# Spectral filter and ELU block on one core: order of the first loads, and new places for weight conversion and sums of x

## The chip, the cores and the metric

One core of a Trainium2 chip. The metric is the device time of one execution in microseconds (us). Engines: PE (TensorE), DVE (VectorE), ACT (ScalarE), POOL (GpSimd), SP (SyncE, which here only issues DMAs).

## The reference, cut to what matters

```python
X = np.fft.rfft(x, axis=1)                  # x: (8, 3008, 256) float32
Y = X * (filt_r + 1j * filt_i)[None]        # filter: (1505, 256)
x = np.fft.irfft(Y, n=3008, axis=1).reshape(24064, 256)
h = x @ w_in                                # w_in: (256, 2048)
g = np.where(h > 0, h, np.exp(np.minimum(h, 0)) - 1)
return g @ w_out                            # w_out: (2048, 256)
```

The weights arrive as 64-bit floats and are turned into float32 by the kernel itself.

## The kernel before, in words

The transforms are matmuls with tables: 3008 = 47 x 64, so a first pass over 64 points (tables `ta`, `tf`), a product with the filter, and the way back (`gs`, `t8`, `tn`). The two weight matrices are used in a seven-product scheme for 2x2 blocks, so sums of weight blocks are needed as well as the blocks.

**Batch 0, up to about 96 us**, has code of its own (L826 to L923). x comes in six pieces `xs[0, c]` (`x_load_first`, L269, SP's queue; pieces 4 and 5 lie in buffers of the pool `t1p`); the table of pieces 2 and 3, and that of 4 and 5, come in one load each. `a_first` (L279) makes the first pass of a piece, `t_first` (L294) transposes for group g of 8, `b_first` (L356) makes group g's spectrum and `products` (L348) multiplies it with the filter `ff` on DVE, `bi_first` (L370) goes back, `y_write_first` (L387) writes to DRAM, and two reads (`y_read_first`, L396) bring it back as `t4f` for `n_first` (L526). The filter is read by `f_read_first` (L323) in four parts: (0,0) and (1,0) on SP's queue, (0,1) and (1,1) on POOL's; groups 0 to 3 need (0,*), groups 4 to 7 (1,*).

**Weights** come in 16 pieces of 512 KB (`w_fetch`, L735), pieces 4q to 4q+3 being quarter q, first two of w_in, then two of w_out. A piece k is converted by `w_split(k)` (two DVE instructions), `w_float(k)` (four ACT instructions, or those numbered: the first needs only the piece, the others the split) and `w_join(k)` (three or four DVE instructions); `w_sums` (four instructions) makes the block sums of a half quarter, on DVE or POOL. `step(k)` is split, float and the join of k-1. The temporary for piece k is `wtmp[WTMP[k]]`. Pieces 5 to 7 are converted beside the filter's groups by the table `BESIDE` (L896): its entry g is put behind group g.

**The rest** is a loop over quads, i = 0, 1, ... (L1025): a quad is one (batch, piece m, weight quarter q) with seven steps up (`up_steps`: matmuls with w_in, copies and ELU) and, for the quad before it, seven down (`down_steps`: matmuls with w_out). The quads start in the order (0,0,0), (0,0,1), (0,1,0..3), (0,0,2), (0,0,3), so quarter q = 1 is needed in quad 1, q = 2 in quad 4, q = 3 in quad 5 (w_out one quad later). Everything else is hung into this loop by hand with `at(quad, place, function, ...)`: place 2 is behind the third step of the first half, place 0 between the halves, place 3 inside the second half, place 1 at the end. Program order is the order in each engine's queue, and no engine passes over a waiting instruction.

Hung in there: pieces 8 to 15 of the weights; `x_load` (SP), `x_unit` (sum and difference of a piece of x, on POOL for batch 1, L223), `a_unit` (the matmuls on them, L234); `f_arrange` (a rearranged copy of the filter in DRAM); `n_unit` and `n_sums` (the last pass and its sums on DVE); `c_unit`, `c_last`, `c_part`, `o_unit` (joining and writing output, DVE and SP).

The steps of piece 4 stand in the code before the first `t_first`:

```python
            step(4)
            w_join(4)
            for k in (5, 6, 7):
                w_fetch(k)
```

Of the kernel before, what the change touches and what calls it, by code (L numbers as in the profile page):

```python
# [32 lines left out]
XC = 4  # L33
# [3 lines left out]
FBUFS = 3  # L37
XSUMS = 6
SUMS = 4
WTMP = (0, 1, 2, 3, 0, 1, 0, 1, 2, 3, 2, 3, 2, 3, 2, 3)  # L40
LO, HI = slice(0, 48), slice(64, 112)
HALVES = slice(0, 64), slice(64, 128)

# [95 lines left out]
def kernel(  # L139
# [47 lines left out]
    edges = glob.tile([P, 2], FP32, name="edges")  # L187
# [547 lines left out]
    def w_fetch(k, queue=nc.gpsimd):  # L735
        q, j = divmod(k, 4)

        if k in (3, 4):
            wd = xp.tile([P, 2, 2, D], FP32, tag="xc", name="wd").rearrange("p k u d -> p (k u d)")
        elif k in (8, 9):  # L740
            wd = t2[:, k - 8].rearrange("p u d -> p (u d)")
        elif k == 13:
            wd = t3s["first"][:, 0].rearrange("p u d -> p (u d)")
        elif k == 15:
            wd = op.tile([P, 16, 2, 32], FP32, tag="o", name="wd").rearrange("p j e s -> p (j e s)")
        else:
            wd = fbufs[{5: 0, 6: 1, 7: 2, 10: 0, 11: 1, 12: 2, 14: 2}.get(k, k)].rearrange("p c u d -> p (c u d)")
        wd = wds[k] = wd.bitcast(U32).rearrange("p (a w) -> p a w", w=2)
        if j < 2:
            srcs = [moe_w_in.bitcast(U32)[ts(j, P), ts(q, 1024)]]  # L750
        else:
            srcs = [moe_w_out.bitcast(U32)[ts(4 * q + 2 * (j - 2) + i, P), :] for i in range(2)]
        for i, s in enumerate(srcs):
            n = 512 // len(srcs)
            queue.dma_start(wd[:, ts(i, n), :].rearrange("p a w -> p (a w)"), s)
# [67 lines left out]
    with tc.manual_schedule():  # L823


        with tc.tile_pool(name="boot", bufs=1) as bp:  # L826
# [18 lines left out]
            for c in (2, 3):  # L845
                x_load_first(c)
            w_fetch(2, nc.sync)
            for c in (4, 5):
                x_load_first(c)
            for z in zt[0] + zt[1]:  # L850
                nc.gpsimd.memset(z.rearrange("p (k r) -> p k r", r=ROWS)[:, :, 48:64], 0.0)
            for gh in range(2):
# [12 lines left out]
            def step(k):  # L865
                w_split(k)
                w_float(k)
                if k > 0:
                    w_join(k - 1)

            nc.sync.dma_start(once, once_d)
            nc.sync.dma_start(gs, gs_d)
            step(0)
            a_first(0)
            step(1)
            a_first(1)
            w_fetch(3)
            w_fetch(4)
            f_read_first(0, 0, nc.sync)
            f_read_first(0, 1, nc.gpsimd)  # L880
            a_first(2)
            step(2)
            a_first(3)
            t4f = xp.tile([P, 2, 2, D], FP32, tag="xc", name="t4f").rearrange("p k u d -> p (k u) d")
            f_read_first(1, 0, nc.sync)
            f_read_first(1, 1, nc.gpsimd)
            step(3)
            a_first(4)
# [41 lines left out]
        n_first(t8)  # L930
        tn_read(0, 1)
        y_read(0, 1)
        for k in (8, 9):
            w_fetch(k, nc.sync)
        for c in range(2):
            x_load(1, c)
        for k in (10, 11, 12, 13):
            w_fetch(k, nc.sync)
        w_fetch(15, nc.sync)

# [6 lines left out]
            plan.setdefault((quad, place), []).append((fn, a))  # L947


        for quad, place, fn, *a in ((0, 0, w_split, 8), (0, 1, w_float, 8),  # L950
                                    (1, 2, w_join, 8), (1, 2, w_split, 9), (1, 0, w_float, 9), (1, 1, w_join, 9),
                                    (1, 1, w_split, 10), (2, 0, w_float, 10),
                                    (2, 1, w_join, 10), (2, 1, w_split, 11), (3, 2, w_float, 11),
                                    (3, 0, w_join, 11), (3, 0, w_split, 12), (3, 1, w_float, 12),
                                    (3, 1, w_join, 12), (4, 2, w_split, 13), (4, 2, w_float, 13), (4, 0, w_join, 13),
                                    (4, 0, w_split, 14), (4, 0, w_float, 14), (4, 1, w_join, 14),
                                    (5, 2, w_split, 15), (5, 2, w_float, 15), (5, 0, w_join, 15),
                                    (1, 1, w_sums, 9, nc.gpsimd), (3, 0, w_sums, 11, nc.gpsimd),
                                    (4, 0, w_sums, 13, nc.gpsimd), (5, 0, w_sums, 15, nc.gpsimd),
                                    (3, 1, w_fetch, 14)):  # L960
            at(quad, place, fn, *a)
        for c in range(2, XBUFS):
            at(c - 2, 0, x_load, 1, c)
# [8 lines left out]
        for b in range(B):  # L972
            t = (b - 1) * PER
            if b > 0:
                for c, s in enumerate((2, 2, 3, 3, 4, 4) if b == 1 else (0, 0, 3, 3, 4, 4)):
                    at(t + s, 0, x_unit, b, c)
# [19 lines left out]
            for m, (s, place, sums) in enumerate(((23, 2, ((23, 0, 0, 1), (23, 3, 2))), (25, 1, ((25, 1),)), (29, 1, ((29, 1),)),  # L996
                                                   (32, 0, ((33, 1),)), (36, 0, ((37, 1),)), (40, 0, ((41, 1),)))):
                if (b, m) == (0, 1):
                    at(0, 1, n_unit, 0, 1)
                    at(0, 1, n_sums, 0, 1)  # L1000
                elif b > 0 or m > 0:
                    r = 21 if m == 0 else s - 2
                    at(t + r, 0, tn_read, b, m)
                    at(t + r, 1 if m == 0 else 0, y_read, b, m)
                    at(t + s, place, n_unit, b, m)

                    for q, p, *a in sums:
                        at(t + q, p, n_sums, b, m, *a)
                if (b, m) == (0, 0):
                    at(3, 0, c_unit, 0, 0)  # L1010
                    at(3, 0, c_last, 0, 0)
                    at(9, 2, c_unit, 0, 0)
                    at(9, 0, c_last, 0, 0)
                    at(9, 0, c_part)
                    at(10, 0, o_unit, 0, 0)
                elif (b, m) == (0, 1):
                    at(7, 0, c_unit, 0, 1)
                    at(8, 0, o_unit, 0, 1)
# [6 lines left out]
        for i in range(-PER, len(items) + 3):  # L1025
# [3 lines left out]
            for n, k in enumerate("DUUDUDDU" if i in opens else "UUDUDDU"):  # L1029
                s = ups if k == "U" else downs  # L1030
                if s:
                    s.pop(0)()
                if n == 2:
                    for fn, a in plan.get((i, 2), ()):
                        fn(*a)
            for fn, a in plan.get((i, 0), ()):
                fn(*a)
# [45 lines left out]
```

## Time and profile before

| what | us |
|---|---|
| three runs: median (lowest to highest) | 2591.99 (2590.68 to 2596.08) |
| profiled execution: its own time | 2595.79 |
| its span, first to last instruction | 2594.0 |
| PE busy of the span | 2526.7 (97%) |
| DVE, ACT, POOL busy | 2064.4, 1538.1, 179.4 |
| 0 to 96 us: PE busy, mean DMA rate | 57.53, 179 GB/s |
| 96 to 196 us: PE busy, DVE busy | 84.44, 76.80 |
| 196 to 250 us: PE busy | 50.69 |

Busy PE is the time in which a matmul is in flight. DMA queue q1 is SP's, q0 POOL's. In timelines a row has start and length in us, engine, line, operation, output<-inputs, shape, and in brackets the idle time of the engine before it and what ended it.

### The profile page before, as it was taken

The numbers are of one execution on the slowest core, as the hardware profiler recorded it, in microseconds if no ns is written. First come the engines' busy times: TensorE is split into PE (matmuls) and PEld (weight loads), VectorE is DVE, ScalarE is ACT, GpSimd is POOL, SyncE is SP. The second block draws the span as 40 slices with busy tenths as digits, with TensorE's granted clock in tenths as the row PEclk, the third lists the DMA queues.
The fourth block names the chain that finished last, engine by engine and source line by source line (L and its number), as shares of the span: only waits on it lengthen the run. The fifth ranks groups of instructions, "written<-read, shape, count | busy, mean of one in ns | idle before, by whom it ended". The sixth has DMA issues, their size and how long they took to land.

```text
span 2594.0 us, 44154 instructions
## 1 busy us (share of the span) xinstructions
PE 2526.7 (97%) x16726; PEld 2161.7 (83%) x16726; DVE 2064.4 (80%) x3609; ACT 1538.1 (59%) x2714; POOL 179.4 (7%) x314
## 2 busy tenths in 40 slices
PE   5889999999999999999999999999999999999998
PEld 4568888888898888988889888898888888898887
DVE  4778887788877888778887888878887788866766
ACT  4575565666556655566556655566556656555554
POOL 3050000001000100000000000000010001000000
PEclk8999999999999999999999999999999999999999
DMA  8662313432135222342314332253313232120010
GB/s 198 186 174 61 82 35 75 120 81 63 28 83 138 68 56 47 87 119 59 76 41 117 81 74 57 50 141 69 72 48 76 72 77 68 31 50 18 19 27 17
DMA packets 228738, 197.23 MB, mean 76 GB/s; under 512 B 128852, under 2 KB 202294, under 8 KB 228334
## 3 DMA queue, kind: packets, MB, share of 16 engines
q1 hardware_dynamic: 215118, 167.42, 26.7%
q0 software_dynamic: 12256, 26.73, 3.9%
q8 instruction: 132, 2.16, 0.4%
q14 instruction: 80, 0.66, 0.1%
q10 hardware_dynamic: 1152, 0.26, 0.1%
HBM read 122.46 MB, written 74.97 MB: 76 GB/s over the span
## 4 chain that ended last, share of the span: by engine, by line
PE 88%; DVE 5%; ACT 2%; DMA 2%; issue 1%; SPq 0%; POOL 0%; DVEq 0%; POOLq 0%; ACTq 0%
PE po L667 41%; PE phs L584 23%; PE phd L584 11%; PE pha L584 6%; PE pse L512 2%; PE pf L411 1%; PE psa L241 1%; PE pv L477 1%; DMA x<-in_x_dram 1%; DVE g L592 1%; DVE g L606 1%; ACT e L602 1%; ACT e L601 1%; DMA t<-tf_t 0%; DMA ff<-in_filt_i_dram 0%
## 5 line engine op out<-in xcount | busy, mean ns | idle before, releaser
L667 PE MATMUL po<-g,wo 128*128 128x256 f32 (+1 forms) x5376 | 1316.9, 377 | 0.0
L667 PEld LDWEIGHTS po<-g,wo 128*128 128x128 f32 x5376 | 1013.7, 190 | 165.4 <-issue 49.7
L595 ACT ACTIVATE g<-phs 128x512 f32<-128x512 f32 (+1 forms) x576 | 338.7, 588 | 717.6 <-PE phs L584 716.6
L584 PE MATMUL phs<-y,wi 128*128 128x256 f32 (+1 forms) x2288 | 580.6, 376 | 5.3 <-ACT g L595 5.3
L602 ACT ACTIVATE e<-e 128x512 f32<-128x512 f32 (+1 forms) x768 | 477.2, 621 | 24.4
L584 PEld LDWEIGHTS phs<-y,wi 128*128 128x128 f32 x2288 | 430.0, 190 | 60.6 <-ACT g L595 8.1
L592 DVE TENSOR_TENSOR g<-phd,g 128x512 f32<-128x512 f32 (+1 forms) x384 | 259.3, 675 | 268.7 <-ACT e L602 196.4
L606 DVE SCALAR_TENSOR_TENSOR g<-e,g 128x512 f32<-128x512 f32 (+1 forms) x576 | 389.4, 676 | 1.5 <-ACT e L602 1.1
L601 ACT ACTIVATE e<-g 128x512 f32<-128x512 f32 (+1 forms) x576 | 353.5, 614 | 62.1 <-DVE g L592 51.1
L606 DVE SCALAR_TENSOR_TENSOR g<-e,phs 128x512 f32<-128x512 f32 (+1 forms) x192 | 129.8, 676 | 145.4 <-ACT e L602 145.4
L584 PE MATMUL phs<-ys,wi 128*128 128x256 f32 (+1 forms) x784 | 198.9, 376 | 4.7 <-ACT g L595 4.7
L584 PE MATMUL phd<-y,wi 128*128 128x256 f32 (+1 forms) x768 | 194.7, 376 | 5.6 <-DVE g L592 5.6
L584 PE MATMUL phd<-ys,wi 128*128 128x256 f32 (+1 forms) x768 | 193.8, 375 | 0.0
L584 PE MATMUL pha<-ys,wi 128*128 128x256 f32 (+1 forms) x752 | 190.0, 375 | 0.0
L601 ACT ACTIVATE e<-phs 128x512 f32<-128x512 f32 (+1 forms) x192 | 113.4, 591 | 112.0 <-PE phs L584 112.0
L584 PEld LDWEIGHTS phs<-ys,wi 128*128 128x128 f32 x784 | 147.8, 190 | 23.2 <-ACT g L595 6.3
L584 PEld LDWEIGHTS phd<-y,wi 128*128 128x128 f32 x768 | 145.0, 190 | 25.5 <-DVE g L592 9.5
L584 PEld LDWEIGHTS phd<-ys,wi 128*128 128x128 f32 x768 | 145.8, 190 | 16.7 <-DVE g L592 0.2
L340 POOL DMA_DIRECT2D fall<-fp x224 | 110.0, 499 | 693.1 <-DVE r L450 690.4
L584 PEld LDWEIGHTS pha<-ys,wi 128*128 128x128 f32 x752 | 142.8, 190 | 16.5
L592 DVE TENSOR_TENSOR g<-pha,g 128x512 f32<-128x512 f32 (+1 forms) x192 | 129.3, 674 | 23.4 <-PE pha L584 23.4
L643 DVE TENSOR_TENSOR g<-g,g 128x512 f32<-128x512 f32 (+1 forms) x192 | 131.7, 686 | 6.7
(181 smaller groups left out, 2163.9 us busy)
## 6 DMA issues: line engine op xcount, KB each, us to landing
t<-yd SPq DMA_DIRECT2D x94, 256.0 KB
z<-t SPq DMA_DIRECT2D x84, 256.0 KB
fall<-fp POOLq DMA_DIRECT2D x224, 96.0 KB, 2.9
t<-z SPq DMA_DIRECT2D x224, 96.0 KB
yd<-t SPq DMA_DIRECT2D x112, 192.0 KB
out_dram<-o SPq DMA_DIRECT2D x632, 32.0 KB
xc<-in_x_dram SPq DMA_DIRECT2D x84, 128.0 KB
xc<-in_x_dram SPq DMA_DIRECT2D x161, 64.0 KB
```

The lines of the kernel that those rows point to most:

```text
L241: nc.tensor.matmul(p[o:o + 64, u, :], w[r, u, o:o + 64], src[r, u, :], start=True, stop=True)
L340: nc.gpsimd.dma_start(t[32 * a:32 * a + 24].rearrange("p c u d -> p (c u d)"), fp[g, a].rearrange("q c u d -> q (c u d)"))
L411: nc.tensor.matmul(pf[p][1][32 * a:32 * a + 32, js, :], fb[r, v, :], t2[r, js, a, :], start=True, stop=True, tile_position=(32 * p, 32 * a))
L512: nc.tensor.matmul(p[o:o + 64, dh, ds(64 * q, n)], t[r, i - 4 * m, ds(dh * P + o, 64)], w[r, i - 4 * m, 0:n], start=True, stop=True)
L584: nc.tensor.matmul(ps[:, a, 0:h], w_in[q][:, COMBO[n], a, :], y[n], start=start and a == 0, stop=True, skip_group_check=True)
L592: nc.vector.tensor_tensor(out=g[o], in0=i0, in1=i1, op=ALU.add)
L595: nc.scalar.activation(out=g[o], in_=i0, func=AXT.Copy)
L601: nc.scalar.activation(out=e, in_=src, func=AXT.Relu, scale=-1.0)
L602: nc.scalar.activation(out=e, in_=e, func=AXT.Exp, scale=-1.0)
L606: nc.vector.scalar_tensor_tensor(out=g[n], in0=es[n], scalar=1.0, in1=src, op0=ALU.subtract, op1=ALU.max)
L643: nc.vector.tensor_tensor(out=b12, in0=b22, in1=b12, op=ALU.subtract)
L667: nc.tensor.matmul(po[i][:, u, 0:h], w_out[q][:, COMBO[n], a, :], g[n][:, a, :], start=begin and a == 0 and n in (1, 3, 6, 4), stop=True, ...
```

## The change

On **POOL**, a copy of one element per partition of x piece 4 is put ahead of POOL's parts of the filter; piece 4 of the weights is fetched behind those, and piece 8 is new behind 5 to 7. On **SP**, piece 3 of the weights and x piece 5 follow x piece 4 and stand ahead of `once`, `gs` and SP's parts of the filter. Piece 4 is converted beside the filter's groups, 5 and 6 later there, 7 and 8 behind them: so pieces 0 to 3 are converted ahead of the filter and 8 ahead of the quads. After the filter SP fetches 9 and 10, two pieces of x, then 11 to 15. In the quads there is a new place 4 (behind step 5, or 4 where a quad starts with a down step), floats are split over places, `x_unit` of batch 1 is called a quad earlier, the sums of piece 15 are on DVE, and some sums and output steps have other places.

```diff
-WTMP = (0, 1, 2, 3, 0, 1, 0, 1, 2, 3, 2, 3, 2, 3, 2, 3)
+WTMP = (0, 1, 2, 1, 0, 1, 0, 1, 0, 3, 2, 3, 2, 3, 2, 3)
...
-            for c in (4, 5):
-                x_load_first(c)
+            x_load_first(4)
...
-            nc.sync.dma_start(once, once_d)
-            nc.sync.dma_start(gs, gs_d)
+            nc.gpsimd.tensor_copy(out=edges[:, 2:3], in_=xs[0, 4][:, XC - 1, 0:1])
             step(0)
             a_first(0)
             step(1)
+            w_fetch(3, nc.sync)
+            x_load_first(5)
+            nc.sync.dma_start(once, once_d)
+            nc.sync.dma_start(gs, gs_d)
             a_first(1)
-            w_fetch(3)
-            w_fetch(4)
             f_read_first(0, 0, nc.sync)
             f_read_first(0, 1, nc.gpsimd)
             a_first(2)
             step(2)
             a_first(3)
-            t4f = xp.tile([P, 2, 2, D], FP32, tag="xc", name="t4f").rearrange("p k u d -> p (k u) d")
+            step(3)
             f_read_first(1, 0, nc.sync)
             f_read_first(1, 1, nc.gpsimd)
-            step(3)
+            w_fetch(4)
+            t4f = xp.tile([P, 2, 2, D], FP32, tag="xc", name="t4f").rearrange("p k u d -> p (k u) d")
             a_first(4)
             a_first(5)
-            step(4)
-            w_join(4)
-            for k in (5, 6, 7):
+            w_join(3)
+            for k in (5, 6, 7, 8):
                 w_fetch(k)
...
-            BESIDE = {2: ((w_split, 5), (w_float, 5, 0, 1)), 3: ((w_float, 5, 2, 3),), 4: ((w_join, 5), (w_float, 6, 0)),
-                      5: ((w_split, 6), (w_float, 6, 1)), 6: ((w_float, 6, 2, 3),), 7: ((w_split, 7),)}
+            BESIDE = {1: ((w_split, 4), (w_float, 4, 0, 1)), 2: ((w_float, 4, 2, 3),),
+                      3: ((w_join, 4),), 4: ((w_split, 5), (w_float, 5, 0, 1)), 5: ((w_float, 5, 2, 3),),
+                      6: ((w_join, 5), (w_split, 6)), 7: ((w_float, 6, 0, 1),), 8: ((w_float, 6, 2, 3),)}
...
+            w_split(7)
             w_join(6)
             w_float(7)
+            w_split(8)
             w_sums(5)
+            w_float(8)
             w_join(7)
             w_sums(7)
+            w_join(8)
...
-        for quad, place, fn, *a in ((0, 0, w_split, 8), (0, 1, w_float, 8),
-                                    (1, 2, w_join, 8), (1, 2, w_split, 9), (1, 0, w_float, 9), (1, 1, w_join, 9),
-                                    (1, 1, w_split, 10), (2, 0, w_float, 10),
-                                    (2, 1, w_join, 10), (2, 1, w_split, 11), (3, 2, w_float, 11),
...
+        early = ((0, 2, w_split, 9), (0, 2, w_float, 9, 0), (0, 4, w_float, 9, 1, 2, 3), (0, 0, w_join, 9), (0, 0, w_split, 10),
+                 (0, 0, w_float, 10, 0, 1), (0, 3, n_unit, 0, 1), (0, 3, w_sums, 9, nc.gpsimd),
+                 (1, 2, n_sums, 0, 1, 0, 1), (1, 2, w_float, 10, 2), (1, 4, n_sums, 0, 1, 2), (1, 4, w_float, 10, 3),
+                 (1, 4, w_split, 11), (1, 4, w_float, 11, 0, 1), (1, 0, w_join, 10), (1, 0, w_float, 11, 2),
+                 (2, 2, w_float, 11, 3), (2, 2, w_split, 12), (2, 4, w_join, 11), (2, 4, w_float, 12, 0, 1), (2, 0, w_float, 12, 2, 3),
+                 (2, 4, w_sums, 11, nc.gpsimd),
+                 (3, 2, w_join, 12), (3, 2, w_split, 13), (3, 4, w_float, 13, 0, 1, 2), (3, 0, w_float, 13, 3),
+                 (4, 2, w_join, 13), (4, 2, w_sums, 13, nc.gpsimd), (4, 2, w_split, 14), (4, 2, w_float, 14, 0),
+                 (4, 4, w_float, 14, 1, 2, 3), (4, 0, w_join, 14), (4, 0, w_split, 15), (4, 0, w_float, 15, 0, 1),
+                 (5, 2, w_float, 15, 2), (5, 4, w_float, 15, 3), (5, 4, w_join, 15), (5, 0, w_sums, 15))
...
+                    elif c % 2 == 0:
+                        for k in (c, c + 1):
+                            at(s - 1, 1 if c else 2, x_unit, b, k)
```

More of the change, by code (lines that the diff above doesn't have):

```diff
@@ L186 @@
     t2 = glob.tile([P, 2, 4, D], FP32, name="t2")
-    edges = glob.tile([P, 2], FP32, name="edges")
+    edges = glob.tile([P, 3], FP32, name="edges")
     fp = fdp.tile([NG, 4, 24, 2, 2, D], FP32, name="fp")
@@ L736, in w_fetch @@
         q, j = divmod(k, 4)
-        if k in (3, 4):
+        if k in (3, 4, 8):
             wd = xp.tile([P, 2, 2, D], FP32, tag="xc", name="wd").rearrange("p k u d -> p (k u d)")
-        elif k in (8, 9):
-            wd = t2[:, k - 8].rearrange("p u d -> p (u d)")
+        elif k in (9, 12):
+            wd = t2[:, 1 if k == 12 else 0].rearrange("p u d -> p (u d)")
         elif k == 13:
@@ L746, in w_fetch @@
         else:
-            wd = fbufs[{5: 0, 6: 1, 7: 2, 10: 0, 11: 1, 12: 2, 14: 2}.get(k, k)].rearrange("p c u d -> p (c u d)")
+            wd = fbufs[{5: 0, 6: 1, 7: 2, 10: 0, 11: 1, 14: 2}.get(k, k)].rearrange("p c u d -> p (c u d)")
         wd = wds[k] = wd.bitcast(U32).rearrange("p (a w) -> p a w", w=2)
@@ L932 @@
         y_read(0, 1)
-        for k in (8, 9):
+        for k in (9, 10):
             w_fetch(k, nc.sync)
@@ L936 @@
             x_load(1, c)
-        for k in (10, 11, 12, 13):
+        for k in (11, 12, 13, 14, 15):
             w_fetch(k, nc.sync)
-        w_fetch(15, nc.sync)
         PER = 24
@@ L947, in at @@
             plan.setdefault((quad, place), []).append((fn, a))
-        for quad, place, fn, *a in ((0, 0, w_split, 8), (0, 1, w_float, 8),
-                                    (1, 2, w_join, 8), (1, 2, w_split, 9), (1, 0, w_float, 9), (1, 1, w_join, 9),
-                                    (1, 1, w_split, 10), (2, 0, w_float, 10),
-                                    (2, 1, w_join, 10), (2, 1, w_split, 11), (3, 2, w_float, 11),
[L954 to L960, printed above, removed]
+        early = ((0, 2, w_split, 9), (0, 2, w_float, 9, 0), (0, 4, w_float, 9, 1, 2, 3), (0, 0, w_join, 9), (0, 0, w_split, 10),
[8 more added lines that the diff above has]
+                 (5, 2, w_float, 15, 2), (5, 4, w_float, 15, 3), (5, 4, w_join, 15), (5, 0, w_sums, 15))
+        for quad, place, fn, *a in early:
             at(quad, place, fn, *a)
@@ L975 @@
                 for c, s in enumerate((2, 2, 3, 3, 4, 4) if b == 1 else (0, 0, 3, 3, 4, 4)):
-                    at(t + s, 0, x_unit, b, c)
+                    if b > 1:
+                        at(t + s, 0, x_unit, b, c)
+                    elif c % 2 == 0:
+                        for k in (c, c + 1):
+                            at(s - 1, 1 if c else 2, x_unit, b, k)
                     if c % 2 == 0:
@@ L997 @@
                                                    (32, 0, ((33, 1),)), (36, 0, ((37, 1),)), (40, 0, ((41, 1),)))):
+                if (b, m) == (0, 2):
+                    sums = ((30, 2, 0, 1), (30, 4, 2))
                 if (b, m) == (0, 1):
-                    at(0, 1, n_unit, 0, 1)
-                    at(0, 1, n_sums, 0, 1)
+                    pass
                 elif b > 0 or m > 0:
@@ L1009 @@
                 if (b, m) == (0, 0):
-                    at(3, 0, c_unit, 0, 0)
-                    at(3, 0, c_last, 0, 0)
+                    at(3, 4, c_unit, 0, 0)
+                    at(3, 4, c_last, 0, 0)
                     at(9, 2, c_unit, 0, 0)
-                    at(9, 0, c_last, 0, 0)
-                    at(9, 0, c_part)
+                    at(9, 2, c_last, 0, 0)
+                    at(9, 4, c_part)
                     at(10, 0, o_unit, 0, 0)
@@ L1017 @@
                     at(7, 0, c_unit, 0, 1)
-                    at(8, 0, o_unit, 0, 1)
+                    at(8, 4, o_unit, 0, 1)
                 else:
@@ L1032 @@
                     s.pop(0)()
-                if n == 2:
-                    for fn, a in plan.get((i, 2), ()):
+                if n == 2 or n == (4 if i in opens else 3):
+                    for fn, a in plan.get((i, 2 if n == 2 else 4), ()):
                         fn(*a)
```

## The prediction

> **What bounds the kernel now.** I read the page's slices first, then the chain of waits, then the timelines of the engines and the DMA queues for the first 260 us, since the change touches nothing later.
>
> ```profile
> PE   5889999999999999999999999999999999999998
> ...
> PEclk8999999999999999999999999999999999999999
> ...
> 18.34 24.23 DMA x<-in_x_dram
> ...
> 42.60 10.23 DMA ff<-in_filt_i_dram
> ```
>
> The first two lines are tenths of 64.9 us slices, the others pieces of the chain (start, length). From about 260 us on TensorE is the bound. Time can be won only before: of 0 to 96 us the table by stretches gives PE 57.53 busy, of 96 to 196 us 84.44, of 196 to 250 us 50.69 of 54. The first stretch stands on loads: x is issued at 18.34, landed at 42.6, then filter.
>
> ```profile
> 13.22 1.38 POOL L755 DMA_DIRECT2D wd<-in_moe_w_out_dram  x2 [4.52 <-PE psa L284]
> ...
> q1 hardware_dynamic: 633, 1.21, 107.4%
> ...
> q0 software_dynamic: 228, 0.80, 54.6%
> q1 hardware_dynamic: 355, 0.68, 51.5%
> ...
> 41.35 3.75 PE L284 MATMUL psa<-t,x 128*128 128x128 f32 x16 [17.45 <-DMA t<-tf_t]
> ...
> 55.11 0.69 DVE L351 TENSOR_TENSOR rq<-psr,ff 128x512 f32<-128x512 f32 x1
> ...
> 79.50 0.68 DVE L354 TENSOR_TENSOR zq<-psi,ff 128x512 f32<-128x512 f32 x1
> ```
>
> The q lines are the DMA view: packets, MB, share; the first is 13.2 to 18 us, the next two 18 to 23 us. SP's queue (q1) moved 1.21 MB in 4.8 us, 253 GB/s, until POOL's loads (q0), issued from 13.22, got packets; then each had about half, and from 23 to 42 us q1 fell to 1.60 MB, 84 GB/s. So x pieces 4 and 5 landed at 41 and 46 us, TensorE stood 17.45 us, and the filter's products run from 55.11 to 80.1 us.
>
> ```profile
> 145.43 1.13 PE L584 MATMUL phs<-y,wi 128*128 128x256 f32 x4 [2.09 <-ACT g L595]
> ...
> 156.50 0.50 PE L241 MATMUL psa<-xc,ta 64*64 64x256 f32 x2 [1.03 <-POOL xc L228]
> ...
> 163.81 0.63 ACT L779 ACTIVATE rq<-rq 128x512 f32<-128x512 uint32 x1 [3.01 <-DVE rq L769]
> ...
> 166.57 1.13 PE L584 MATMUL phs<-y,wi 128*128 128x256 f32 x4 [2.67 <-ACT g L595]
> ...
> 174.95 1.76 DVE L642 TENSOR_TENSOR g<-g 128x512 f32<-128x512 f32 x1
> ```
>
> In the quads PE stands for two things: ACT's copies queued behind a float step that waits for DVE's split (3.01, then PE's 2.67), and GpSimd's sums of x, issued just ahead of the matmuls that use them.
>
> **Part 1, loads.** Removed from the road of x: w3 and w4 (1.05 MB on q0) and GpSimd's half of the filter (1.54 MB; in both kernels behind w3/w4 or alone), held by a 128x1 copy that waits for x piece 4. Queued behind that copy on POOL are twelve filter DMAs, w4 and w5 to w8; nothing else until the sums of quad 0. SP alone carries, up to x piece 4, 5.14 MB (w0 to w2, five x, four tables), 4.16 of which it had moved by 18 us; 0.98/253 GB/s puts it at 22, taken 24 for the slowest engine. Then the last tables, w3 and x piece 5 follow on SP, 1.55 MB more: 28 to 29. POOL's first packets came 4.8 us after its first issue, so from about 28 q0 competes only with once, gs and f(0,0): with f(0,1) 1.87 MB at some 200 GB/s (20 to 40 us gave 235 and 185), 9.4 us: the first half of the filter is there at about 38, taken 39 to 40. The x path beside it: last matmuls from 29 (3.50 each piece), copies, transposes and ACT's 2.04 us, as 46.26 to 55.11 took 8.85 with a float step of 2.82 between: 36 to 37. Products start at 40, 15 earlier.
>
> By the Trainium skill, "DMA: Bandwidth & Descriptors", "Latency and other measured facts", a GpSimd DMA's first byte comes after about 1 us; by that figure the half would start some 4 us sooner and the sum be about 2 us better. This trace shows 4.8 and 12.2 us to landing (filter, POOL), so I keep those.
>
> **Part 2, the filter stage.** w4 now lies behind both filter halves on POOL: 2.06 MB into q0. Before, q0 moved 2.06 MB in about 16.4 us (cumulated over windows), with faster rows first; I take 18.5 from 28, so 46.5, bounds 43 and 50. Its split stands behind two groups' products, at 40+4.8 = 45: DVE and ACT stand 1.5 us. After it DVE has 24 products at 0.60 (14.4), joins of w4 and w5 (0.60+0.72+0.61 each, 3.9), splits (w4, w5, w6 at 0.67, 2.0) and about 1 of waits: 46.5+21.3 = 67.8, against 80.1: **-12.3, taken -12** (bounds -16 and -5). Without w4's cover each us of lateness costs one. w3's float ahead of a_first(4) waits for 27, before x piece 5, and is hidden; the join is done by 33.
>
> Behind the last product come split 7, join 6, split 8, sums 5, join 7, sums 7, join 8. In before this tail ended at 89.4 and the next DVE work was at 95.35, after the y round trip (issue 84.93, t4f read 89.83, PE 92.75). w8 adds split 0.76, join 1.94 and waits for floats (1.46 between the last two ACT copies, and 2.6): end 92.7 in before's clock. Cost 0; if the round trip were 3 us shorter, up to 3 would show. w5 to w8 (2.1 MB) meet the y writes; the t3f buffers are two deep, cost 0 to 2, included in the bounds.
>
> **Part 3, quads 0 and 1.** w8 is gone from here: split 0.76, join 1.94, float 2.6. But w9's float now stands in quad 0, whose steps are a chain PE, ACT, DVE with nothing beside. Its first part (0.67) waits on ACT for w9, which should land as w8 did, at 100.4, where DVE already waited 1.27: the copy at 99.33 moves to 101.0 (+1.7). The other parts (2.0) and half of w10's (1.2) stand ahead of later copies and exponentials; the gap of 3.05 (PE at 110.13, behind w8's float and two y copies) stays in another form. I put quad 1's s6 at 111.5, **+1.4**, and another +1 for split 11 behind n_sums in DVE's backlog. w9, w10 and w11 to w15 are on SP ahead of x_load(1,2): w14, moved from POOL, adds 0.52 MB or 2.1 us to x piece 2, needed 30 us later; 0.
>
> **Part 4, quads 1 to 7.** PE's idle pieces from 111 to 206 us sum to 11.8: GpSimd's sums 4.8 (1.21, 1.03, 2.56), float behind split 5.3 (2.09, 2.67, 0.53), DVE 1.37, rest 0.32. With the sums of x a quad (12 us) ahead, the first go; splits stand further ahead of their floats, so most of the second. DVE has per quad 6.7 of its 12.1 us; the five quads give 27 free us against 15.4 of conversion left, 1.7 (w15's sums now 4x0.43 on DVE, POOL's 3.1 gone), n_sums 2.4, joins of output 3. I leave 4 us: -7.8. With +2.4: **-5.4** (bounds -10 and +4). Output steps moved from place 0 to 2 and 4 around quads 3, 8 and 9: up to 1 us (DVE's 1.09 add ahead of a 1.12 wait at 243.17), taken -0.5.
>
> Against this part speaks a row: the L642 above took 1.76 where others take 0.69, beside GpSimd's sum of x (174.36 to 176.17). Summed over 126 to 190 us such excesses are about 9.4 us of DVE. The same 12 sums remain, in quads with more conversion. The Trainium skill, "SBUF — State Buffer", "Who interferes with whom", says that a DVE instruction with two SBUF inputs and a GpSimd one that reads SBUF block each other for a whole instruction; the trace agrees with 1.76 against 0.69. By that rule alone moving saves nothing.
>
> **Sum.** -12 -5.4 -0.5 = -17.9 on the profiled execution's 2595.8 (span 2594.0): 2577.9. That execution is 3.8 above the median 2592.0, so I forecast 2592.0-17.9 = **2574** there.
>
> **Rivals.** (A) More: w4 comes with the need and all waits of part 4 go: -16-9 = -25, 2567. For: q0's rate. Against: DVE's load. (B) It doesn't bring x forward, because the late x is SP's own small rows and not q0: products start at 53, the w4 work in the stage costs what is gained, part 4 stays: 2586. Against: 253 to 84 GB/s as q0 starts. (C) The port: conversions meet GpSimd's sums on the path, quads +2 to +4 instead of -5.4: about 2582. (D) **w4 takes the place of the wait removed**: ACT's and DVE's queues stand whole for it. Price 1 us per us after 46.5; even at 64.4, slower by over 0.2% from 69.6; at 72 it is 2600. For: it is last of POOL's thirteen DMAs held since 24, each 10 to 12 us to landing. Against: q0's 4.15 MB took 31.5 us from 18.
>
> **Chances.** Forecast 0.50 (own range 2569 to 2580), A 0.12, B 0.08, C 0.14, D 0.16 (0.06 of it within 0.2%). 0.2%, some 5.2 us, is about what a measurement here can tell from no change. Faster: 0.50+0.12+0.14 and half of B, 0.80; within: half of B and 0.06, 0.10; slower 0.10. The range, 2565 to 2587, goes from just below A to just above B and leaves out D and a part of B, 0.2.
>
> **What would show it.** x piece 4's matmuls at 24 to 28 instead of 41.35; products' first row at 40; split 4 waiting under 3 us for its DMA; last product at 68; the y round trip unchanged; PE idle in the next 100 us down from 15.5 to about 10, with no gap named POOL. Wrong would be: POOL's filter landing after 50, a DVE wait over 10 us for w4, or ACT waiting for w9 over 3 us in quad 0.

## The result and the profile after

The changed kernel took 2585.49 us (median of seven runs, 2580.81 to 2585.88), the kernel before 2592.49 in the same comparison. The ratio of the two is 0.9965, 95% interval 0.9953 to 0.9977: about 9 us faster by the ratio, 7 by the two medians. I had forecast 2574, 18 faster. The sign was right and the time lies inside the range, but half of the gain or more did not come. The profiled execution took 2585.88 against 2595.79, so the -9.9 between the two traces is what must be explained.

First the slices of the page after. Only the first digits of the first row differ from before. Quads 6 to 8 (from 184.61 us after, 194.01 before) have the same lengths, quad 9 is 0.3 us shorter, and all later slices read alike.

```profile
PE   6789999999999999999999999999999999999998
PEclk8999999999999999999999999999999999999999
```

The chain of waits after (start, length, what). x is off GpSimd's traffic: on the chain it lands at 24.1. GpSimd's copy into `edges` waits for it and starts at 24.15 (the last row here, from POOL's timeline), and the filter follows.

```profile
14.61 9.49 DMA x<-in_x_dram
...
25.98 8.93 DMA ff<-in_filt_r_dram
36.69 8.09 DMA ff<-in_filt_i_dram
...
24.15 0.68 POOL L870 COPY edges<-x 128x1 f32<-128x1 f32 x1 [15.45 <-DMA x<-in_x_dram]
```

By its issue time the row at 36.69 is one of POOL's loads of the second half of the filter. Groups 0 to 3 need the first half. POOL's share of its imaginary part was issued by 28.4 and took 9.8 to 10.2 us to landing; SP's share was issued from 28.25 on, and the profile has no landing times for it. So it is probably SP's share that came at 44.7, which no row shows.

The DMA queues after (packets, MB, share), 18 to 23, 23 to 28 and 28 to 33 us. Until 28 SP's queue has the engines alone and moves 256 and 290 GB/s, where it had 136 and 72 before; then the two share. From 28 to 43 us they moved 3.03 MB, 1.72 of them on POOL's queue.

```profile
q1 hardware_dynamic: 751, 1.28, 109.9%
...
q1 hardware_dynamic: 791, 1.45, 105.1%
...
q1 hardware_dynamic: 418, 0.60, 54.7%
q0 software_dynamic: 207, 0.53, 54.3%
```

The timelines of PE and DVE after, up to the last pass of batch 0.

```profile
25.42 2.02 PE L284 MATMUL psa<-t,x 128*128 128x128 f32 x16 [1.89 <-ACT wi L291]
...
38.69 0.69 DVE L351 TENSOR_TENSOR rq<-psr,ff 128x512 f32<-128x512 f32 x1 [4.72 <-DMA ff<-in_filt_r_dram]
44.76 0.69 DVE L352 TENSOR_TENSOR rq<-psr,ff 128x512 f32<-128x512 f32 x1 [5.38 <-DMA ff<-in_filt_i_dram]
45.59 1.94 PE L345 MATMUL psr<-tf,once 48*64 48x512 f32 x2 [7.57 <-DVE rq L352]
48.95 0.42 DVE L769 TENSOR_SCALAR wm<-wd 128x512 uint32<-128x512 uint32 x1
...
74.96 0.68 DVE L354 TENSOR_TENSOR zq<-psi,ff 128x512 f32<-128x512 f32 x1
85.91 3.14 PE L535 MATMUL psn<-t,t4f 128*128 128x128 f32 x16 [4.65 <-DMA t4f<-yd]
```

x piece 4's matmuls moved from 41.35 to 25.42 and the first product from 55.11 to 38.69, but the second product waits 5.38 us for the filter's imaginary part; PE stands 7.57 us and takes 1.94 us for two matmuls that take 1.07 at 43.29 in the kernel e11 below. The last product came 4.54 earlier (79.50 to 74.96), the last pass 6.84 (92.75 to 85.91).

The table by stretches, of before, 36 to 52 us, and then of after, 40 to 60. The columns are stretch, length, busy time of PE, PEld, DVE, ACT and POOL, granted clock, DMA share, GB/s.

```profile
36.00:40.00 4.00, 0.00 (x0) 0.00 (x0) 3.28 (x8) 0.00 (x0) 2.12 (x4) 0.50 1.06 187
40.00:44.00 4.00, 2.65 (x12) 2.68 (x13) 0.00 (x0) 0.57 (x2) 0.00 (x0) 0.50 1.05 296
44.00:48.00 4.00, 2.84 (x14) 2.58 (x13) 0.00 (x0) 0.75 (x3) 0.00 (x0) 0.50 0.84 248
48.00:52.00 4.00, 3.54 (x26) 3.23 (x25) 0.00 (x0) 2.86 (x7) 0.00 (x0) 0.83 0.44 86
```

```profile
40.00:44.00 4.00, 0.00 (x0) 0.00 (x0) 0.00 (x0) 0.00 (x0) 1.08 (x2) 0.77 1.05 196
44.00:48.00 4.00, 2.41 (x10) 1.16 (x13) 3.24 (x6) 0.00 (x0) 1.58 (x3) 0.50 1.02 245
48.00:52.00 4.00, 4.00 (x26) 2.20 (x19) 2.99 (x6) 1.31 (x2) 0.00 (x0) 0.50 0.97 310
52.00:56.00 4.00, 4.00 (x23) 2.24 (x24) 1.29 (x2) 3.43 (x6) 0.00 (x0) 0.52 0.73 250
56.00:60.00 4.00, 4.00 (x38) 1.65 (x33) 3.08 (x6) 2.24 (x5) 0.00 (x0) 1.00 0.26 70
```

Before, the clock was at half too, but while TensorE waited for x; it was back before the products began at 55.11. After, it is the filter that TensorE waits for, and groups 2 and 3 run at half clock: 23 to 26 matmuls in 4 us where 38 fit at 56. The Trainium skill, "TensorE: Matmul & The Clock Gate", "What's actually happening", says that about 3.4 us without work halve the clock and about 3.4 us of work restore it. The first agrees with 0.50 behind the 7.57 us, but below the clock also falls behind waits of 2.53, 2.02 and 1.18 us. The second doesn't agree: PE worked from 45.59 to 55.8 at half.

Then the quads after, in ACT's, PE's, DVE's and POOL's timelines.

```profile
92.84 0.67 ACT L779 ACTIVATE rq<-t 128x512 f32<-128x512 uint32 x1 [1.89 <-DMA t<-in_moe_w_in_dram]
...
101.39 1.26 POOL L227 TENSOR_TENSOR sd<-xc 128x512 f32<-128x512 f32 x1
101.40 1.74 DVE L606 SCALAR_TENSOR_TENSOR g<-e,g 128x448 f32<-128x448 f32 x1
102.73 1.53 POOL L228 TENSOR_TENSOR xc<-xc 128x512 f32<-128x512 f32 x1
103.06 1.69 DVE L642 TENSOR_TENSOR g<-g 128x448 f32<-128x448 f32 x1
...
112.33 0.63 ACT L779 ACTIVATE rq<-rq 128x512 f32<-128x512 uint32 x1 [5.64 <-DVE rq L769]
113.45 1.51 PE L584 MATMUL phs<-y,wi 128*128 128x224 f32 x4 [4.75 <-ACT g L595]
```

The early sums of x lie beside DVE's steps, which take 1.7 us; DVE falls behind, the split of piece 11 is late, ACT stands 5.64 us for it and PE 4.75 for ACT's copy. The seven traces that have these quads (after, e1, e5, e6, e7, e9, e10) all show that wait of ACT, 5.64 to 5.66 us; in e3, with the sums later, it is 1.75.

The gain by stages of the two traces: last pass -6.84; from it to quad 0's second step up (4.72 to 4.30) -0.42; from there to quad 8's (121.4 to 119.3) -2.1; output steps in quad 9 (15.76 to 15.44) -0.3. Together -9.7 of the -9.9. The quads by length, each from the first matmul of its second step up to that of the next quad:

| us | quad 0 | 1 | 2 | 3 | 4 | 5 | 0 to 7 |
|---|---|---|---|---|---|---|---|
| before | 7.9 | 15.7 | 17.8 | 20.5 | 21.4 | 13.2 | 121.4 |
| after | 11.7 | 18.0 | 14.6 | 19.3 | 18.4 | 12.4 | 119.3 |

Quads 6 and 7 are the same (13.9, 10.9).

### The profile page after: what moved, and what is told of

Its sections match the earlier page's. It is cut to its first block, busy times and chain, and to the rows that moved or that the text cites. A ratio compares the mean times of both kernels' runs of the same rounds, so it can differ in the third digit from the quotient of the medians.

```text
span 2584.1 us, 44148 instructions
## 1 busy us (share of the span) xinstructions
PE 2526.8 (98%) x16726; PEld 2163.6 (84%) x16726; DVE 2070.1 (80%) x3613; ACT 1536.9 (59%) x2714; POOL 177.0 (7%) x308
## 3 DMA queue, kind: packets, MB, share of 16 engines
q1 hardware_dynamic: 215550, 167.95, 26.7%
## 4 chain that ended last, share of the span: by engine, by line
PE 89%; DVE 6%; DMA 2%; ACT 2%; issue 1%; SPq 0%; POOL 0%; DVEq 0%; ACTq 0%; POOLq 0%
PE po L667 41%; PE phs L584 23%; PE phd L584 12%; PE pha L584 6%; PE pse L512 2%; PE psa L241 1%; PE pf L411 1%; PE pv L477 1%; DVE g L606 1%; DVE g L592 1%; ACT e L602 1%; PE po L345 0%; ACT e L601 0%; DVE g L643 0%; DVE g L642 0%
## 5 line engine op out<-in xcount | busy, mean ns | idle before, releaser
L584 PE MATMUL phs<-y,wi 128*128 128x256 f32 (+1 forms) x2288 | 582.4, 377 | 10.3 <-ACT g L595 10.3
L584 PEld LDWEIGHTS phd<-ys,wi 128*128 128x128 f32 x768 | 146.6, 191 | 17.8 <-DVE g L592 1.4
```

Source lines behind the costliest of these rows:

```text
L584: nc.tensor.matmul(ps[:, a, 0:h], w_in[q][:, COMBO[n], a, :], y[n], start=start and a == 0, stop=True, skip_group_check=True)
```

## The experiments

After this, my theory had two parts: TensorE's clock made the filter stage slow, and GpSimd's early sums with piece 9's place ate what the new deal saves in the quads. Rivals: the lateness of piece 4, ACT's queue, and shared DMA bandwidth. Each is an edit of the changed kernel; "stage" is the time from the end of group 0's products to the end of group 7's. e1, e6, e9 and e11 add matmuls whose result nobody reads (the profile counts each of them twice).

The filter's landing differs from one profiled execution to the next though the load code is the same (group 0's products end between 43.0 and 51.1 us in the eleven traces with after's loads), and with it the start of the last pass, by some 2 us either way. So I compare stages and quads in single traces, and ratios in runs. The quads vary too: the seven traces with after's quads took 118.9 to 120.3 us, the two with e2's 115.7 and 117.1.

| kernel | median us | ratio to before, 95% | last pass starts, us | quads 0 to 7, us |
|---|---|---|---|---|
| after | 2585.49 | 0.9965 (0.9953 to 0.9977) | 85.91 | 119.3 |
| e1 | 2590.17 | 0.9988 (0.9979 to 0.9998) | 92.79 | 120.3 |
| e2 | 2582.60 | 0.9964 (0.9950 to 0.9978) | 83.96 | 117.1 |
| e3 | 2584.52 | 0.9970 (0.9959 to 0.9980) | 87.91 | 117.2 |
| e4 | 2585.08 | 0.9975 (0.9966 to 0.9985) | 83.12 | 120.6 |
| e5 | 2596.88 | 1.0014 (1.0005 to 1.0024) | 95.75 | 120.3 |
| e6 | 2583.49 | 0.9967 (0.9954 to 0.9980) | 82.72 | 120.1 |
| e7 | 2587.16 | 0.9979 (0.9970 to 0.9988) | 85.60 | 120.0 |
| e8 | 2586.17 | 0.9977 (0.9967 to 0.9986) | 86.83 | 120.8 |
| e9 | 2584.62 | 0.9963 (0.9949 to 0.9977) | 86.87 | 119.5 |
| e10 | 2584.20 | 0.9964 (0.9951 to 0.9977) | 81.27 | 118.9 |
| e11 | 2579.37 | 0.9950 (0.9935 to 0.9965) | 79.97 | 115.7 |
| e12 | 2583.85 | 0.9967 (0.9956 to 0.9979) | 84.44 | 119.95 |

### The loads: e5 and e7

e5 takes the copy away, so that POOL's filter loads start early again.

```diff
-            nc.gpsimd.tensor_copy(out=edges[:, 2:3], in_=xs[0, 4][:, XC - 1, 0:1])
```

> The kernel after without GpSimd's copy of one element of x, so that its filter loads are issued as soon as its fills are done. Theory (its queue takes half of the DMA engines from SP's): x pieces 4 and 5 reach TensorE at 33 to 41 us instead of 25.4 and 29.5; the fourth weight piece lands earlier than 48; group 0's products end within 3 us of after's 46.6, since the same bytes stand ahead of them; total within 2 us of after or up to 3 slower. Rival (the late x is SP's own small rows): x pieces as in after, within 2 us.

PE's timeline of e5: x pieces 4 and 5 are about as late as before the change (41.35 and 46.26 there).

```profile
39.77 3.76 PE L284 MATMUL psa<-t,x 128*128 128x128 f32 x16 [6.93 <-DMA t<-tf_t]
```

The last pass starts 9.8 us later than with the copy, and the ratio is 1.0014 (1.0005 to 1.0024): without its one-element copy the change gains nothing and may lose a little. By the two ratios the copy is worth 0.49%, 12.7 us; by the two medians 11.4. Rival B (x late by SP's own rows) falls. My expectation was about right on x and wrong on its price: I had the time at most 3 us above after's, and group 0's products within 3 us of 46.6, and they ended at 58.3.

e7 makes POOL's second half of the filter, and the weights behind it, wait for the first half (`edges` gets two more columns for it).

```diff
             f_read_first(0, 1, nc.gpsimd)
+            nc.gpsimd.tensor_copy(out=edges[0:48, 3:5], in_=ff[0:48, 1, 0, :, 0])
```

> The kernel after with a second small copy on GpSimd, which reads SP's first filter part and stands behind GpSimd's first, so that its second filter part and weight pieces 4 to 8 are issued only when the first half of the filter is there. Theory (the queues share; what GpSimd loads ahead of need delays SP's part): group 0's products end at 41 to 44 instead of 46.6, the fourth piece lands at 52 to 56 instead of 48.3 and stalls split 4 for 6 us or more, so the last product ends 2 to 5 us later than after's 75.6. Rival (SP's part is late by its own small rows, not by sharing): group 0's products within 1.5 us of after.

Group 0's products end at 41.2 instead of 46.6, but the split of piece 4 moves from 48.95 to 50.91, having waited 7.35 for its load, TensorE waits 6.17 us there instead, and the last product ends at 76.0 (after: 75.6). 41.2 lies below all eleven traces with after's loads, so the first half does suffer from the sharing; but the bytes are the same, and here holding some back only moved the wait.

### The clock: e1, e6, e9, e10

Three kernels keep TensorE busy while the filter is awaited; the scratch tile lies in a free PSUM buffer.

```diff
             for g in range(NG + 2):
+                if g == 2:
+                    warm = psO.tile([P, 128], FP32, tag="po2", name="warm")
+                    for k in range(40):
+                        nc.tensor.matmul(warm, w_in[0][:, 0, 0, :], w_in[0][:, 1, 0, :], start=True, stop=True)
```

This is e6; e1 has 16 of 128x512, e9 18 of 128x128.

> The kernel after, with 16 matmuls of 128x512 whose result nobody reads, on TensorE between the spectrum of group 1 and that of group 2, where it stood 7.57 us for the filter (38.0 to 45.6) and then worked to about 56 us at a granted clock of 0.50 to 0.52. Theory (the late filter also let the clock fall): the clock stays near 1.00 from 45 to 56 us, the last product ends at 71 to 72.5 instead of 75.6, the last pass starts at 82 to 83 instead of 85.9, the time falls by 3 to 4 us. Rival (VectorE and the fourth weight piece bound the stage, the clock does not): the clock rises and the last product moves by less than 1 us.

> The kernel after with 40 matmuls of 128x128 (4.4 us at full clock, result unused) on TensorE ahead of group 2's spectrum; the earlier try took 14 us there and ran over the wait. Theory (the clock that fell in the wait lengthens groups 1 to 3): granted clock 1.00 through 45 to 56 us, end of group 0's to end of group 7's products 25 to 26 us instead of 29.0, total 2 to 4 us faster than after. Rival (the fourth weight piece or VectorE sets this stretch): it stays 28 us or more.

> The kernel after with 18 of the small matmuls instead of 40. The 40 took 9.2 us (39.9 to 49.1, 115 ns a pass, two passes each) where the wait had ended at 43; but behind them groups 2 and 3 ran at a clock of 1.00 at a pace of 3.75 us, against 8.5 and 4.6 us in the kernel after. Theory (half of TensorE's clock costs 5 us there): 18 end before the filter comes, clock 1.00, group 0's to group 7's products 25 to 26.5 us instead of 29.0 (after) and 30.7 (40 matmuls), total 2 to 4 us faster than after. Rival (the fourth piece at 47 to 48 sets the start of group 2 anyway): 28 us or more.

PE's timeline of e1, then of e6: the added matmuls took 14.00 and 9.20 us, longer than the wait.

```profile
44.89 14.00 PE L905 MATMUL warm<-wi 128*128 128x512 f32 x32 [0.25 <-ACT tf L303]
```

```profile
39.94 9.20 PE L905 MATMUL warm<-wi 128*128 128x128 f32 x80 [0.25 <-ACT tf L303]
```

In both the clock stayed at 1.00, but the groups stood behind them: group 2's products end 11.0 and 8.2 us behind group 1's. Both were too big, a fault of the experiments. e9 fitted the size, but in its profiled execution the filter came late (group 0 at 48.4); its matmuls ended at 44.8, TensorE then stood 2.53 us and the clock fell all the same. Its timeline and its table by stretches:

```profile
47.29 1.62 PE L345 MATMUL psr<-tf,once 48*64 48x512 f32 x2 [2.53 <-DVE rq L352]
```

```profile
44.00:48.00 4.00, 1.47 (x9) 0.76 (x8) 1.46 (x3) 0.00 (x0) 2.12 (x4) 0.96 1.04 296
48.00:52.00 4.00, 4.00 (x26) 2.52 (x27) 3.49 (x7) 1.30 (x2) 0.00 (x0) 0.50 1.03 289
52.00:56.00 4.00, 4.00 (x24) 2.50 (x22) 2.58 (x4) 1.77 (x4) 0.00 (x0) 0.50 0.66 230
```

The stage was 29.1 us, as in after (29.0). So e9 alone settles nothing, except that a wait of 2.53 us was enough for the clock to fall here.

e10 tests the rival: piece 4 is converted behind group 2 instead of group 1.

```diff
-            BESIDE = {1: ((w_split, 4), (w_float, 4, 0, 1)), 2: ((w_float, 4, 2, 3),),
...
+            BESIDE = {2: ((w_split, 4), (w_float, 4, 0, 1)), 3: ((w_float, 4, 2, 3),),
+                      4: ((w_join, 4),), 5: ((w_split, 5), (w_float, 5, 0, 1)), 6: ((w_float, 5, 2, 3),),
+                      7: ((w_join, 5), (w_split, 6)), 8: ((w_float, 6),)}
```

> The kernel after with the conversion beside the filter one group later: split of piece 4 behind group 2, piece 6's float whole behind group 8. Theory (with the filter there at 44 to 47, the fourth piece at 48 is no longer what stands, and TensorE's clock is): the products' stage within 1.5 us of after's 29.0, total within 2 us of after. Rival (the fourth piece's wait on VectorE and ScalarE is the term that was too small): 25 to 27 us, total 2 to 4 us faster.

Its stage was 25.4 us, 3.6 shorter, which by itself speaks for the rival. But its table by stretches shows that the clock was low only from 44 to 48:

```profile
44.00:48.00 4.00, 3.94 (x29) 3.04 (x30) 2.81 (x5) 0.00 (x0) 1.58 (x3) 0.57 1.03 258
48.00:52.00 4.00, 4.00 (x39) 1.76 (x33) 3.11 (x7) 3.13 (x6) 0.00 (x0) 1.00 0.95 301
```

So e10 changed both and does not tell them apart. Its ratio (0.9964) is that of after (0.9965). The rival stands so far; e11 below bounds its share. As to ACT's queue, no wait of DVE in after from 49 us to the last product names ACT, though such names are inferred.

### The quads: e2, e3, e4, e8, e12

e2 keeps the new loads and filter stage and has the old deal in the quads (piece 8 stays ahead of them, sums of x at their old places, output steps too); e3 puts back only the places of the sums of x; e8 is e2 with the sums of x at their new places; e12 is e2 with piece 8 converted in quads 0 and 1 again and no longer ahead of them.

```diff
-                    if b > 1:
-                        at(t + s, 0, x_unit, b, c)
-                    elif c % 2 == 0:
-                        for k in (c, c + 1):
-                            at(s - 1, 1 if c else 2, x_unit, b, k)
+                    at(t + s, 0, x_unit, b, c)
```

This is e3 (and the sums' part of e2). The old deal of e2, cut, and e12's addition:

```diff
+        early = ((1, 2, w_split, 9), (1, 0, w_float, 9), (1, 1, w_join, 9),
+                 (1, 1, w_split, 10), (2, 0, w_float, 10),
...
+        early = ((0, 0, w_split, 8), (0, 1, w_float, 8), (1, 2, w_join, 8), (1, 2, w_split, 9), (1, 0, w_float, 9), (1, 1, w_join, 9),
...
```

> The kernel after with the new loads and the filter stage, but in the quads the old places of conversion (without piece 8, which is done), of the sums of x, of the last pass and of the output steps. Theory (the new places lose in quads 0 and 1 what they win in 2 to 5): start of the last pass as after, 85.9; quad 0 about 8 us instead of 11.7, quad 1 about 15 instead of 18.0, quads 2 to 5 up to 8 us longer than after; total within 2 us of the kernel after. Rival (the new places are what wins in the quads): 4 to 8 us slower than after.

> The kernel after with only the sums of x back at their old places, a quad later. Theory (GpSimd's sums in quad 0's and 1's chain hold VectorE: four of its instructions took 1.6 to 1.7 us from 101 to 108): quads 0 and 1 together 3 to 4 us shorter than after's 29.7, quads 2 to 4 together 4 to 6 us longer, since TensorE waits for the sums again; total 0 to 3 us slower than after. Rival (the float steps of pieces 9 and 10 alone lengthen quads 0 and 1): these two stay within 1 us.

> The second kernel of this study (new loads, old deal of conversion in the quads) with the early sums of x of the kernel after. From quad 0's second step to quad 8's it took 117.1 us with late sums, the kernel after 119.3, the kernel after with late sums 117.2. Theory (early sums hold VectorE in quads 0 and 1, and give less back): 118 to 120 us. Rival (early sums help where VectorE has less conversion beside them): 113 to 116 us.

> The second kernel of the study with piece 8 converted in quads 0 and 1 again, at its old places: new loads, and the deal of the kernel before as it was. Theory (what the quads win is piece 8 taken out of them, not the new places): quads 0 to 8 take 120.5 to 122 us, as before's 121.4, against 117.1 without it; quad 1 15 to 16 us instead of 11.5. Rival (the quads won for another reason, such as the loads): within 1.5 us of 117.1.

Quads 0 to 7: e12 119.95, e2 117.1, so piece 8's absence gives -2.9 (-4.2 against e11, which has e2's quads and 115.7). Quad 1 is 4.1 shorter without it; e2's quad 4 is 1.6 longer than e11's and e12's, and its clock was at half for 3.4 us there. e8 took 120.8, so early sums on the old deal cost 3.7; after 119.3, e3 117.2, so on the new deal they cost 2.1. Quads 2 and 4 gain from them (14.6 and 18.4 in after, 18.0 and 21.9 in e3), quads 1, 3 and 0 pay (18.0, 19.3, 11.7 against 12.6, 16.6, 10.7). DVE's timeline of e3 shows steps like those at 101.40 and 103.06 of after, now with nothing of GpSimd beside them; the last row is ACT's wait for the split of piece 11:

```profile
103.20 0.63 DVE L606 SCALAR_TENSOR_TENSOR g<-e,g 128x448 f32<-128x448 f32 x1
103.74 0.62 DVE L642 TENSOR_TENSOR g<-g 128x448 f32<-128x448 f32 x1
...
110.23 0.63 ACT L779 ACTIVATE rq<-rq 128x512 f32<-128x512 uint32 x1 [1.75 <-DVE rq L769]
```

0.62 against 1.69: the rule that I quoted from the Trainium skill ("SBUF — State Buffer", "Who interferes with whom") agrees. In runs, the ratios of e2, e3 and e12 are not apart from that of after: 2 us are at the edge of what they can tell. So what the quads' parts cost is read from traces alone.

e4 gives quads 0 and 1 a plain deal (piece 9 whole at the middle and end of quad 0, 10 in quad 1) and leaves the rest new.

```diff
-        early = ((0, 2, w_split, 9), (0, 2, w_float, 9, 0), (0, 4, w_float, 9, 1, 2, 3), (0, 0, w_join, 9), (0, 0, w_split, 10),
...
+        early = ((0, 0, w_split, 9), (0, 1, w_float, 9), (0, 1, n_unit, 0, 1), (0, 1, n_sums, 0, 1),
+                 (1, 2, w_join, 9), (1, 2, w_split, 10), (1, 0, w_float, 10), (1, 0, w_sums, 9, nc.gpsimd),
```

> The kernel after with pieces 9 and 10 (and the split of 11), the last pass of piece 1 and its sums dealt over quads 0 and 1 as pieces 8 and 9 were before; everything from quad 2 on and the early sums of x stay. Theory (float steps and the wait for piece 9 in quad 0's chain cost there): quad 0 about 8 us instead of 11.7, quad 1 15 to 17 instead of 18.0, quads 2 to 5 as after, total 4 to 6 us faster than after. Rival (the sums of x on the shared port are the cost): quad 0 stays above 10 us, total within 1.5 us.

Quads 0 and 1 are 8.3 and 15.5 instead of 11.7 and 18.0, but quad 2 is 22.5 instead of 14.6: the sum is 120.6. The work was moved, not saved, and the 4 to 6 us that I expected did not come.

### Together: e11

e11 is e2's deal with e9's 18 matmuls and e10's table.

> New loads, the old deal in the quads without piece 8 (second kernel of the study), 18 small matmuls, and the conversion beside the filter one group later. If the terms add up: last pass starts at 80 to 82, quads 0 to 8 take 117 us, total 2577 to 2580. If the wait for the filter or the fourth piece sets the stage whatever the clock: 2582 to 2583, as the second kernel.

Its PE timeline and its table by stretches:

```profile
37.99 4.29 PE L905 MATMUL warm<-wi 128*128 128x128 f32 x36 [0.25 <-ACT tf L303]
43.29 1.07 PE L345 MATMUL psr<-tf,once 48*64 48x512 f32 x2 [1.01 <-DVE rq L352]
```

```profile
44.00:48.00 4.00, 3.87 (x38) 2.62 (x38) 4.00 (x8) 0.64 (x2) 1.05 (x2) 1.00 1.06 284
48.00:52.00 4.00, 4.00 (x36) 1.77 (x33) 3.60 (x8) 3.36 (x7) 0.00 (x0) 1.00 0.92 300
52.00:56.00 4.00, 4.00 (x37) 1.87 (x40) 2.67 (x6) 2.55 (x5) 0.00 (x0) 1.00 0.76 273
```

Here TensorE stood only 1.01 us, the clock stayed at 1.00 and the stage was 23.8 us. From the end of group 1's products to the last one took 21.4 us; in after, with the clock at half up to 55.8, 26.6. These 5.2 are not the clock's alone, for e11 has another table too, with one split and one join less ahead of the last product. e1 and e6 have after's table and a clock of 1.00. So I compare from the end of group 2's products to the last one, in after, e1 and e11 (columns as above):

```profile
53.46:75.64 22.18, 21.44 (x176) 8.37 (x174) 17.37 (x32) 16.14 (x30) 0.00 (x0) 0.95 0.45 118
...
63.32:83.42 20.10, 19.36 (x171) 7.58 (x160) 17.38 (x32) 15.55 (x30) 0.00 (x0) 1.00 0.48 118
...
49.21:68.26 19.05, 18.11 (x160) 7.49 (x156) 15.66 (x28) 13.40 (x25) 0.00 (x0) 1.00 0.58 176
```

The clock costs 2.1 us here and the table 1.05. e6 gives 20.1 as e1 does, and e12, with after's table, no added matmuls and a clock of 1.00 from 52.3 on, 20.2. Between groups 1 and 2 it is 4.4 against 2.4 in e11, of which the split of piece 4, which e11 has later, takes 0.67. So the clock's share of the 5.2 is at least 2.1 and at most about 3.5, and the rest is the table's. e12 agrees: from group 1 to the last product it took 24.1.

Four runs of e11 gave 2576.71 to 2582.59, median 2579.37, the lowest of all kernels: 0.9950 of before. Against after the intervals overlap (0.9935 to 0.9965, 0.9953 to 0.9977), though the medians are 6.1 us apart: that e11 is faster than after is likely and not shown.

## Where the prediction held and where it failed

By the stages above, 8.2 us of the 17.9 that I had summed up did not come. Part 2 lacks 7.5 and the quads 3.3; 2.3 in the tail and 0.4 ahead of quad 0 came on top.

- **Part 1 was right for x and wrong for the filter.** "24 for the slowest engine" was 24.15, and x piece 4's matmuls came at 25.42, inside 24 to 28. e5 shows that the copy does it. The first product came at 38.69, forecast 40, but it needs only the real part. The imaginary part of the half that I had at "39 to 40" came at 44.7. The rate was right (182 to 225 GB/s from 28 to 43 us, taken 200), the bytes were not: the 1.87 MB leave out the second half and the weights on POOL's queue, which moved 1.72 MB in that time where its first half is 0.77. In e7, with the second half held back, group 0's products ran from 38.68 on without a wait for the filter.
- **Part 2 is the step that failed**: "46.5+21.3 = 67.8, against 80.1: -12.3, taken -12". The last product came 4.54 earlier. It ended at 75.64, 7.8 us behind 67.8. About 2.4 of these lie ahead of split 4, which began at 48.95 instead of 46.5; piece 4 was there by then, but the first two groups' products had waited for the filter. The other 5.4 are in the stage, which I made of DVE's instructions and "about 1 of waits" (21.3 us; 26.7 measured). DVE waited for TensorE's matmuls instead. At least 2.1 and at most about 3.5 of the 5.4 are TensorE's clock at half; the rest DVE waits at full clock as well (e1: 20.1 us from group 2 on, 17.4 of them busy). I had shown the 8 at the head of the granted clock and not asked which stretch it stood for, nor where a new wait would put it. The mechanism (products begin earlier, the end follows) was right; the terms for the filter's landing and for the stage were too small, and so the gain was too big.
- **The tail**, taken 0, gave 2.3: from the last product's end to the last pass 10.3 us instead of 12.6. I had priced this case ("if the round trip were 3 us shorter, up to 3 would show") and not forecast it; why it was shorter is open.
- **Part 3 was mis-sized**: +2.4 forecast, +6.0 measured (3.76 and 2.28). ACT waits for piece 9 until 92.84, as I said; what I left out is that the early sums slow DVE in just these quads, so that the wait for split 11 came to 5.64 us (1.75 in e3) and PE's gap in quad 1 to 4.75 where I expected the old 3.05.
- **Part 4 was about right in size, not in its parts**: quads 2 to 5 -8.2, forecast -7.8. PE's gaps named POOL are gone, as I said; those behind ACT's floats are not (2.62 at 145.03, 2.37 at 163.27; before 2.09 and 2.67), where I had said most would go. PE's idle time in these quads fell by 5.0 (11.9 to 6.8); the other 3.2 are in its busy time (quad 2: 14.63 of busy against 16.23, with 93 matmuls in both), for which I have no row. Behind the gaps of 4.75 and 2.62 the clock also went to half for 3.4 us, from 113.8 and from 144.6. And the price lay in quads 0 and 1: rival C's mechanism, GpSimd's sums that hold DVE's steps, is what e3 and e8 show. With both, the quads gave -2.1 where I had -5.4, and e2 and e11 against e12 show that piece 8 alone gave -2.9 to -4.2. That the new deal as a whole costs some 2 us or more against the old one rests on traces (118.9 to 120.3 in seven, 115.7 and 117.1 in two); the runs don't exclude zero.
- **Output steps**: -0.3, forecast -0.5.
- **Rival D** (piece 4 takes the place of the wait) did not happen: split 4 waited for nothing in after. Where the filter came earlier it did wait: 0.94 us in e4, 2.00 in e6, 3.08 in e2, 7.35 in e7.

Left open: how much work in a step of the clock brings it back (from the end of the wait to 1.00 it took 5 us in e10, 10 in after), and why the filter's landing differs by up to 8 us between executions of one load order.

## What to carry to other kernels

When a change brings a transfer forward, ask which engine will stand waiting for the next one, and read the granted clock there: a wait of TensorE just ahead of its dense work is paid for twice, once as the wait and once at half clock. Hold back loads that are not yet needed by a dependency on those that are; it costs one instruction, and without it there was no gain here. But where what is held back is needed next, as in e7, the wait only moves. Count in a load's landing what the other queue moves beside it, needed or not. Price a step moved off a gap together with what it will lie beside: sums on GpSimd put beside two-input steps on DVE cost at least as much as the waits that they removed.

## What the runs showed of the hardware

TensorE's clock came down behind waits of 2.53 us (e9), 2.02 us (e10) and 1.18 us (e5, at 59.6), not behind 1.01 us (e11). PE's timeline and two stretches of e5:

```profile
57.25 1.04 PE L345 MATMUL psr<-tf,once 48*64 48x512 f32 x2 [1.18 <-DVE rq L352]
...
59.00:60.00 1.00, 1.00 (x17) 0.83 (x13) 1.00 (x2) 0.00 (x0) 0.00 (x0) 0.80 0.23 73
60.00:61.00 1.00, 1.00 (x13) 0.85 (x8) 1.00 (x4) 0.00 (x0) 0.00 (x0) 0.50 0.02 6
```

Back at 1.00 it was only after some 5 to 11 us in which matmuls were in flight nearly all the time. Worked out from the granted clock of stretches of 1 us (a share of the stretch at 1.00, the rest at 0.50), the changes in one trace lie whole steps of 3.41 us apart: in after it fell at 18.3, 42.2, 86.5, 113.8 and 144.6 and was back at 21.7, 55.8, 89.9, 117.3 and 148.0. So the time at half comes in steps and does not follow the length of the wait alone (6.8 us behind 1.18 in e5 and behind 5.51 in e12): in the filter stage 3.4 us in e10, 6.8 in e2, e3, e5 and e12, 10.2 in e7 and e9, 13.7 in after, e4 and e8. Which step a wait falls into differs between executions, and e11's 1.01 us lay across the end of one. A load queue that is not urgent took about half of the bandwidth: SP's queue moved 290 GB/s alone (23 to 28 us after) and 120 GB/s beside POOL's (28 to 33 us, 0.60 MB, POOL's 0.53).
